# Late stores, longer rings and streamed filler operands in a four-layer training step

## The chip, the cores and the metric

The kernel runs on one core of a Trainium2 chip. The metric is the device time of one launch in microseconds (us). All executions used here are of the fast state; the program uses one core. Times are medians of the executions.

Engine names: PE is TensorE (matmul), PEld its weight loads, DVE is VectorE, ACT is ScalarE, POOL is GpSimd, SP is SyncE, which issues the loads. A `q` behind a name (SPq) is that engine's sequencer.

## The reference, cut to what matters

One forward and one backward pass over four residual layers: linear attention, gated GLU, linear attention, gated GLU. Sequence 2048, width 512, GLU width 1376, bf16. Both attention layers share weights, and both GLU layers do.

```python
x = x + A(layernorm(x), wqkv, wo)             # layer 0
x = x + B(layernorm(x), w_gate, w_up, w_down) # layer 1
x = x + A(layernorm(x), wqkv, wo)             # layer 2
x = x + B(layernorm(x), w_gate, w_up, w_down) # layer 3
# A: phi(t) = where(t > 0, t + 1, exp(t)) + 1e-6, 32 heads of 16
#    kv = phi(k)^T v;  z = sum phi(k);  o = phi(q) kv / (phi(q) z + 1e-6);  y = o @ wo
# B: h = sigmoid(x @ w_gate) * (x @ w_up);  y = h @ w_down
out, vjp = jax.vjp(f, x, wqkv, wo, w_gate, w_up, w_down);  grads = vjp(grad_out)
```

## The kernel before

The kernel works in blocks of four 128-row tiles (512 rows), four blocks in all. Its stages, in order: first attention forward (a key loop, then a query phase), first GLU forward, second attention forward, a fused forward and backward of the last GLU, backward attention 2, backward of the first GLU, backward attention 0, and the final weight gradients. In the backward stages, weight gradients of layers already finished serve as *filler*: their matmuls have low priority and go where TensorE would wait.

Three parts matter. First, the key loop. A pair tile `pkst` (ring of 2) feeds a transposing transfer into `pkT`, of which there is only one; the store of `pkT` is issued by GpSimd in program order:

```python
k.work, k.p_pq, k.p_st, k.p_M = pool("work", 2), pool("pq", 2), pool("stage", 2), pool("M", 1)
...
    if st % 2 == 0:
        k.pkst = k.p_st.tile([P, 2, D], BF16, name="pkst")
    ...
    if j == 0:
        k.pkT = k.p_st.tile([P, NB, NDC, P], BF16, name="pkT", bufs=1)
    if st % 2:
        nc.sync.dma_start_transpose(out=k.pkT[:, j - 1:j + 1]..., in_=flat(k.pkst))
    if j == NB - 1:
        k.st.dma_start(out=sv["pkT"][b], in_=flat(k.pkT))       # k.st is GpSimd
```

Second, the query phase. It divides by the denominator as exp(-ln d). VectorE makes `qp`, GpSimd makes `rp`, and GpSimd issues the stores of `qp`, `rp` and of the transposed `qn`:

```python
nc.scalar.activation(ld[:], d_ps[:], ACT.Ln, bias=k.eps[:])
nc.scalar.activation(rd[:], ld[:], ACT.Exp, scale=-1.0)
nc.vector.tensor_tensor(qp[:, dc, :], pq[:, dc, :], rd[:], ALU.mult)
nc.gpsimd.tensor_tensor(rp[:, dc, :], eq[:, dc, :], rd[:], ALU.mult)
```

Third, the filler weight gradients. Each sum over 16 row tiles needs a natural operand (`g_all` or `h_all`, kept whole in memory, 2 MB) and a transposed one (`set_t`, loaded block by block through a transposing transfer):

```python
def mid2():
    k.g3 = load_all(k, sv[3]["g"], "g_all"); wd3(SETS[0:1])
def mid0():
    dw_cols(k, "wqkv", D, (0, D), [(k.h2, sv[2]["dkT"])], "first")
    k.h3 = load_all(k, sv[3]["h"], "h_all")
a_bwd(k, 2, False, hi, mid2)
wd3(SETS[1:])
k.h2 = load_all(k, sv[2]["h"], "h_all")
with hi():
    b_bwd(k, 1)
dw_cols(k, "wqkv", 0, (0, D), [(k.h2, sv[2]["dqT"])], "first")
a_bwd(k, 0, True, hi, mid0)
...
for st, t in pieces(k, src, c0, w):            # t: a set_t tile's rows
    for ic in range(NDC):
        matmul(ps[ic], lhsT=h[:, st, ic * P:(ic + 1) * P], rhs=t, ...)
```

Of the kernel before, what the change touches and what calls it, by code (L numbers as in the profile page):

```python
# [16 lines left out]
D = 512  # L17
# [38 lines left out]
def kernel(  # L56
# [60 lines left out]
    k.A = {l: {} for l in (0, 2)}  # L117

# [55 lines left out]




class LN:
# [11 lines left out]
    def one(self, st):  # L190
# [12 lines left out]
        nc.gpsimd.tensor_tensor(rstd, rstd, k.neghalf[:], ALU.pow)  # L203
# [8 lines left out]
        if j == NB - 1:  # L212
            k.st.dma_start(out=by_tile(k.sv[l]["h"], b * NB, NB), in_=self.h[b][:])
            if l % 2 == 0:
                k.st.dma_start(out=k.sv[l]["hT"][b], in_=flat(self.hT[b]))
# [11 lines left out]
def forward(k):  # L227
    nc, tc = k.nc, k.tc
    with ExitStack() as ctx:
# [19 lines left out]
        b_both(k, 3, lns[3])  # L249

# [42 lines left out]
def a_fwd(k, l, ln, nxt):  # L293
    with ExitStack() as ctx:
        pool = lambda name, bufs, **kw: ctx.enter_context(k.tc.tile_pool(name=f"{name}{l}", bufs=bufs, **kw))
        k.work, k.p_pq, k.p_st, k.p_M = pool("work", 2), pool("pq", 2), pool("stage", 2), pool("M", 1)
# [14 lines left out]
def a_fwd_body(k, l, ln, nxt):  # L311
# [10 lines left out]
    def keys(st):  # L322
        b, j = divmod(st, NB)
        hT = ln.hT[b][:, j]
        if st % 2 == 0:
            k.pkst = k.p_st.tile([P, 2, D], BF16, name="pkst")
# [8 lines left out]
        pk = k.pkst[:, st % 2, :]  # L335
        pks.append((pk, nc.vector.scalar_tensor_tensor(pk, k_ps[:], 1.0 + EPS, a_t[:], ALU.add, ALU.max)))  # L336
        if j == 0:
            k.pkT = k.p_st.tile([P, NB, NDC, P], BF16, name="pkT", bufs=1)
        if st % 2:
            nc.sync.dma_start_transpose(out=k.pkT[:, j - 1:j + 1].rearrange("p a c q -> p (a c) q"), in_=flat(k.pkst))  # L340
        if j == NB - 1:
            k.st.dma_start(out=sv["pkT"][b], in_=flat(k.pkT))
# [58 lines left out]
    for b in range(NBLK):  # L401
        pq, eq = qb[b]
        qp = qps[b] = k.p_st.tile([P, NDC, SB], BF16, name="qp_t")
        rp = k.p_st.tile([P, NDC, SB], BF16, name="rp_t", bufs=1)
        for dc in range(NDC):
# [7 lines left out]
            nc.gpsimd.tensor_tensor(rp[:, dc, :], eq[:, dc, :], rd[:], ALU.mult)  # L413
        k.st.dma_start(out=sv["qp"][b], in_=flat(qp))
        k.st.dma_start(out=sv["rp"][b], in_=flat(rp))
        qn = k.p_st.tile([P, NDC, NB, P], BF16, name="qn_t", bufs=1)
        nc.sync.dma_start_transpose(out=qn[:].rearrange("p c a q -> p (c a) q"), in_=flat(qp))
        k.st.dma_start(out=sv["qn"][b], in_=flat(qn))
        if b + 2 < NBLK:
            qb.append(q_block(k, ln.hT[b + 2]))  # L420
        if b:
            out(b - 1)
    out(NBLK - 1)

    k2_ps = k.ps.tile([P, NDC, P], F32, name="kv_ps", tag="bank")
    for c in range(NDC):
        mm4(k, k2_ps[:, c, :], lambda ic: Eb(ic, c), lambda ic: wv(ic, c))
    nc.vector.tensor_tensor(kv[:], k2_ps[:], mask4, ALU.mult)
    MT = k.keep.tile([P, NDC, D], BF16, name=f"MT{l}")
    for jc in range(NDC):  # L430
        m_ps = k.ps.tile([P, D], F32, name="MT_ps", tag="bank")
        for c in range(NDC):
            nc.tensor.matmul(m_ps[:, c * P:(c + 1) * P], lhsT=k.wo[:, c, jc * P:(jc + 1) * P], rhs=kvT[:, c, :],
                             start=True, stop=True)
        (nc.vector.tensor_copy if jc % 2 else nc.scalar.copy)(MT[:, jc, :], m_ps[:])
    A.update(nz=nz, kv=kv, MT=MT)


def b_fwd(k, l, ln, nxt):
    nc, sv = k.nc, k.sv[l]  # L440
    with ExitStack() as ctx:
# [12 lines left out]
        for b in range(NBLK):  # L454
            ln.need(b * NB + NB - 1)
            hT = ln.hT[b]
            hhT = hhs[b] = p_hh.tile([P, NFC, SB], BF16, name="hhT_t")
            for f0, nf in FGRP:
                s4 = p_s.tile([P, 4, SB], BF16, name="s_t")
                for fc in range(f0, f0 + nf):  # L460
# [8 lines left out]
                    if fc == 3:  # L469
                        ln.need((b + 2) * NB - 1)  # L470
# [5 lines left out]
        down(NBLK - 1)  # L476


def b_both(k, l, ln):

    nc, sv = k.nc, k.sv[l]
    with ExitStack() as ctx:
# [3 lines left out]
        hhs, dds, gns, gTs = {}, {}, {}, {}  # L486

        def grads(b):
            gns[b] = k.p_h.tile([P, NB, D], BF16, name="gn_t", tag="h_t")
            nc.sync.dma_start(out=gns[b][:], in_=by_tile(k.g_in, b * NB, NB))  # L490
            gTs[b] = k.p_hT.tile([P, NDC, SB], BF16, name="gT3_t", tag="hT_t")
            nc.sync.dma_start_transpose(out=gTs[b][:], in_=k.g_in[rows(b * NB, NB), :])
# [12 lines left out]
        grads(0)  # L505
        for b in range(NBLK):
# [3 lines left out]
            for fc in range(NFC):  # L510
# [28 lines left out]
                if fc == 3 and b + 1 < NBLK:  # L539
                    grads(b + 1)  # L540
                    ln.need((b + 2) * NB - 1)
# [24 lines left out]
def backward(k):  # L566
    nc, tc = k.nc, k.tc
    with ExitStack() as ctx:
# [3 lines left out]
        k.small = pool("bsmall", 6, side="right")  # L572
        k.p_all = pool("dw_all", 2, side="right")
# [394 lines left out]
```

## Time and profile before

The kernel before takes 1333.15 us (three runs, 1331.93 to 1333.93).

| what | value | view |
|---|---|---|
| span of the profiled run | 1334.9 us | page |
| TensorE busy | 1128.9 us | page, busy list |
| all matmuls at the warm pace | about 1038 us | worked out, see below |
| mean granted clock | 0.932 | cores |
| DMA traffic | 236.25 MB, mean 177 GB/s | page |

The page's busy list, and its slices. Each slice is 1/40 of the span, each digit a busy share in tenths; PEclk is the clock granted to TensorE in tenths, DMA the mean share of the 16 transfer engines.

```profile
PE 1128.9 (85%) x5254; PEld 514.1 (39%) x5344; DVE 606.8 (45%) x1103; ACT 390.6 (29%) x769; POOL 388.9 (29%) x548
PE   3675789988579999998789769888978978899997
PEclk9888799998789999999889799988989989999999
DMA  9846554464778334146964898454575568976994
```

TensorE is busy 85% of the span, with low digits in the first five slices and again in slices 11 and 12: these are the two attention forwards. The next lines are two of GpSimd's waits from 16 to 137 us (who waited for whom, us in total, times, longest).

```profile
POOL sv_pkT_109 L342 <- DMA pkT<-pkst: 19.3, 2, 11.3
POOL sv_qn_112 L418 <- DMA qn_t<-qp_t: 16.6, 3, 11.4
```

GpSimd stands 19.3 us in front of stores whose source, a transposed tile, has not landed, and 16.6 us in front of stores of `qn`. VectorE waits too, for the transfer that still reads `pkst` (VectorE's waits, 16 to 75 us):

```profile
DVE pkst L336 <- DMA pkT<-pkst: 12.6, 3, 5.0
```

In the query phases the table of windows gives busy time by engine: us of the window, then busy us and instruction counts of PE, PEld, DVE, ACT and POOL, the granted clock, the DMA share and GB/s.

```profile
74.00:137.00 63.00, 39.91 (x194) 17.54 (x196) 45.15 (x87) 30.65 (x51) 27.64 (x34) 0.84 0.53 142
316.00:372.00 56.00, 40.02 (x200) 17.88 (x202) 44.85 (x86) 30.38 (x51) 25.21 (x31) 0.85 0.69 188
```

Last, a piece of the chain of waits in the GLU backward (start, us, what). "Issue" is time in which the profile shows nothing being waited for; VectorE's next step, at 819.02 us, stands behind it.

```profile
792.15 26.88 issue
```

### The profile page before, as it was taken

What the parts mean: (1) busy time and instruction counts of PE and PEld (TensorE: products, weight loads), DVE (VectorE), ACT (ScalarE), POOL (GpSimd) and SP (SyncE); (2) the same over time, 40 slices, a digit from 0 to 9 for tenths busy, and PEclk for the clock granted to TensorE, in tenths of its full rate; (3) what the DMA queues carried; (4) which work ended last, traced back from release to release, by engine and by line L of the source; (5) the groups of instructions that cost most, each with busy time, mean ns of one, the idle gap of its engine ahead of it and who ended that gap; (6) DMA issues with size and microseconds to landing.
All of it is one profiled execution on the core that took longest, in us unless ns stands there. A gap on an engine that the chain in (4) does not pass through costs nothing. (4 is left out here: it accounts for less than half of the span.)

```text
span 1334.9 us, 14969 instructions
## 1 busy us (share of the span) xinstructions
PE 1128.9 (85%) x5254; PEld 514.1 (39%) x5344; DVE 606.8 (45%) x1103; ACT 390.6 (29%) x769; POOL 388.9 (29%) x548
## 2 busy tenths in 40 slices
PE   3675789988579999998789769888978978899997
PEld 1232333433234444443344324333434433345543
DVE  6277465446774545445547411555634851000011
ACT  1153321214535335243212532545221340000000
POOL 7134343211565344241320142334132111000111
PEclk9888799998789999999889799988989989999999
DMA  9846554464778334146964898454575568976994
GB/s 267 239 142 142 142 164 139 160 177 110 220 183 245 95 124 131 61 144 155 279 209 156 217 237 256 154 179 133 151 212 198 195 155 176 232 168 135 235 252 114
DMA packets 377420, 236.25 MB, mean 177 GB/s; under 512 B 290945, under 2 KB 352193, under 8 KB 377345
## 3 DMA queue, kind: packets, MB, share of 16 engines
q1 hardware_dynamic: 355968, 163.32, 49.5%
q0 software_dynamic: 21376, 71.97, 14.9%
q8 instruction: 42, 0.69, 0.2%
q14 instruction: 34, 0.27, 0.1%
HBM read 69.60 MB, written 94.50 MB: 123 GB/s over the span
## 5 line engine op out<-in xcount | busy, mean ns | idle before, releaser
L920 PE MATMUL dw_ps<-set_t,h_all 128*128 128x512 bf16 (+1 forms) x1006 | 210.0, 366 | 10.1 <-DMA set_t<-sv_ddT_130 4.4
L920 PEld LDWEIGHTS <-h_all 128*128 128x128 bf16 x1024 | 100.6, 99 | 115.4 <-issue 16.4
L891 DVE TENSOR_TENSOR dw_new<-dw_ps,dw_old 128x512 bf16<-128x512 f32 (+1 forms) x27 | 17.4, 686 | 221.4 <-PE dw_ps L920 151.5
L159 PE MATMUL g_ps<-hT_t,wg 128*128 128x512 bf16 x352 | 96.8, 399 | 13.1 <-DMA hT_t<-h_t 8.3
L159 PE MATMUL dhh_ps<-gT_t,wdT 128*128 128x512 bf16 x339 | 93.0, 394 | 14.0 <-ACT dhh_t L681 5.6
L159 PE MATMUL u_ps<-hT_t,wu 128*128 128x512 bf16 x352 | 94.8, 392 | 0.0
L893 ACT CAST dw_new<-dw_ps 128x512 bf16<-128x512 f32 (+2 forms) x51 | 26.5, 573 | 222.3 <-PE dw_ps L920 107.1
L683 DVE TENSOR_TENSOR dd_t<-dhh_t,sh_t 128x1024 bf16<-128x1024 bf16 x44 | 40.7, 938 | 110.4 <-ACT dhh_t L681 39.9
L894 POOL DMA_DIRECT2D out_dram<-dw_new x51 | 27.5, 542 | 213.9 <-ACT dw_new L893 122.0
L654 PE MATMUL dh_ps<-wuT,dd_t 128*128 128x512 bf16 x169 | 65.9, 391 | 20.1 <-ACT t_sb L622 16.0
L934 PE MATMUL dw_ps<-g_all,set_t 128*128 128x512 bf16 (+1 forms) x342 | 79.3, 383 | 4.2 <-ACT dw_new L893 2.0
L521 POOL TENSOR_TENSOR sd_t<-hh_t,oms 128x512 bf16<-128x512 bf16 x44 | 51.8, 1178 | 92.1 <-DVE hh_t L520 74.6
L724 POOL TENSOR_TENSOR dqT_t<-w_t,rp_l 128x512 bf16<-128x512 bf16 x32 | 37.5, 1188 | 128.1 <-DVE w_t L723 51.3
L654 PE MATMUL dh_ps<-wgT,dd_t 128*128 128x512 bf16 x173 | 67.2, 389 | 0.4
L353 PE MATMUL E_ps<-pkst,h_t 128*128 128x512 bf16 x125 | 40.4, 455 | 27.2 <-DVE pkst L336 27.2
L654 PEld LDWEIGHTS <-dd_t 128*128 128x128 bf16 x352 | 35.0, 100 | 65.5 <-issue 24.4
L527 DVE TENSOR_TENSOR dd_t<-dhh_t,sd_t 128x1024 bf16<-128x1024 bf16 x44 | 34.9, 798 | 53.1 <-POOL sd_t L521 53.1
L159 PEld LDWEIGHTS <-wdT 128*128 128x128 bf16 x352 | 35.4, 101 | 59.0 <-issue 20.6
L159 PEld LDWEIGHTS <-wg 128*128 128x128 bf16 x352 | 35.7, 102 | 58.3 <-issue 20.7
L159 PEld LDWEIGHTS <-wu 128*128 128x128 bf16 x352 | 35.7, 101 | 45.5 <-issue 7.0
L934 PEld LDWEIGHTS <-set_t 128*128 128x128 bf16 (+1 forms) x352 | 35.3, 101 | 46.3 <-issue 7.6
L465 ACT ACTIVATE s_t<-g_ps 128x512 bf16<-128x512 f32 x44 | 25.7, 598 | 87.9 <-PE g_ps L159 74.9
(608 smaller groups left out, 1974.8 us busy)
## 6 DMA issues: line engine op xcount, KB each, us to landing
sv_ddT_130<-dd_t SPq DMA_DIRECT2D x40, 256.0 KB, 2.2
sv_ddT_116<-dd_t SPq DMA_DIRECT2D x40, 256.0 KB, 2.5
out_dram<-dw_new POOLq DMA_DIRECT2D x42, 128.0 KB, 3.8
sv_hhT_115<-hhT_t POOLq DMA_DIRECT2D x4, 1280.0 KB, 6.1
sv_hhT_129<-hh_t POOLq DMA_DIRECT2D x40, 128.0 KB, 2.2
sv_s_118<-s_t POOLq DMA_DIRECT2D x8, 512.0 KB, 4.7
out_dram<-o_t POOLq DMA_DIRECT2D x16, 256.0 KB, 2.5
sh_t<-sv_s_118 SPq DMA_DIRECT2D x8, 512.0 KB, 5.1
```

Source lines behind the costliest of these rows:

```text
L159: i = k.nc.tensor.matmul(out, lhsT=lhs(c), rhs=rhs(c), start=(c == 0), stop=(c == n - 1))
L353: nc.tensor.matmul(E_ps[ic][:], lhsT=h[:, ic * P:(ic + 1) * P], rhs=pk, start=(st == 0), stop=(st == NST - 1))
L465: k.last_sigmoid = nc.scalar.activation(s4[:, fc - f0, :], g_ps[:], ACT.Sigmoid)
L521: nc.gpsimd.tensor_tensor(sd[:, 1, :], hh[:], oms[:], ALU.mult)
L527: mul = nc.vector.tensor_tensor(dd[:], dhh[:].unsqueeze(1).to_broadcast([P, 2, SB]), sd[:], ALU.mult)
L654: nc.tensor.matmul(acc[b][j][:], lhsT=dd[:, a, rows(j)], rhs=(k.wuT, k.wgT)[a][:, fc, :], start=(fc == 0 and a == 0), stop=(fc == NFC - 1 ...
L683: nc.vector.tensor_tensor(dd[:], dhh[:].unsqueeze(1).to_broadcast([P, 2, SB]), sh[:, :, i, :], ALU.mult)
L724: nc.gpsimd.tensor_tensor(dqT[:, dc, :], w_t[:], rp[:, dc, :], ALU.mult)
L893: nc.scalar.copy(new[0:r, 0:w], ps)
L894: k.st.dma_start(out=dst, in_=new[0:r, 0:w])
L920: k.nc.tensor.matmul(ps[ic][:, 0:w], lhsT=h[:, st, ic * P:(ic + 1) * P], rhs=t, start=(i == 0 and st == 0), stop=(i == len(srcs) - 1 and s ...
L934: k.nc.tensor.matmul(p[0:r, :], lhsT=t[:, f:f + r], rhs=g[:, st, :], start=(i == 0 and st == 0), stop=(i == len(srcs) - 1 and st == NST - 1))
```

## The change

Its intent, in four parts:

1. Key tiles, transposed keys, `qp`, `rp` and `qn` come from one ring of 7 tiles of 4 KB per partition, not from rings of 2 and 1.
2. A store of a transposed tile (`pkT`, `hT`, `qn`) is put later in GpSimd's program order, behind four more of its reciprocal products or layer-norm steps, so GpSimd does useful work while the transpose lands. The small products of the attention (`kv`, `MT`) move into the query loop, and layer norms and output gradients are asked for earlier.
3. In the backward stages `qp`, `rp` and the GLU's `s`/`hhT` loads share one ring `sh` that lives through all stages; `dqT` has two tiles in place of one.
4. The filler gradients no longer keep a whole natural operand: both operands are streamed block by block through a ring of 6 set tiles. Filler is cut into smaller pieces and none is left inside the GLU backward. The staging ring grows from 2 to 3. For the final gradients the ring of set tiles stays at 6, where before it had 8 there.

```diff
+def pooled(k, ins):
+    k.n_pool += 1
+    while k.waiting and k.waiting[0][0] <= k.n_pool:
+        after(k, k.st.dma_start(**k.waiting.pop(0)[1]), ins)
+def store_later(k, lag=4, **kw):
+    k.waiting.append((k.n_pool + lag, kw))
 ...
-    k.work, k.p_pq, k.p_st, k.p_M = pool("work", 2), pool("pq", 2), pool("stage", 2), pool("M", 1)
+    k.work, k.p_pq, k.p_st, k.p_M = pool("work", 2), pool("pq", 2), pool("stage", 7), pool("M", 1)
 ...
-            k.st.dma_start(out=sv["pkT"][b], in_=flat(k.pkT))
+            store_later(k, out=sv["pkT"][b], in_=flat(k.pkT))
 ...
-        rp = k.p_st.tile([P, NDC, SB], BF16, name="rp_t", bufs=1)
+        rp = k.p_st.tile([P, NDC, SB], BF16, name="rp_t", tag="st")
 ...
-            nc.gpsimd.tensor_tensor(rp[:, dc, :], eq[:, dc, :], rd[:], ALU.mult)
+            pooled(k, nc.gpsimd.tensor_tensor(rp[:, dc, :], eq[:, dc, :], rd[:], ALU.mult))
 ...
-        k.p_all = pool("dw_all", 2, side="right")
-        k.p_set, k.p_dst, k.p_ln = mpool("dw_set", 4), mpool("dw_stage", 2), mpool("lnb", 2)
+        k.p_set, k.p_dst = pool("dw_set", 6), pool("dw_stage", 3)
+        k.p_sh, k.p_ln = mpool("sh", 2), mpool("lnb", 2)
 ...
+        wd3 = lambda i: dw_rows(k, "wd", SETS[i], [(sv[3]["g"], sv[3]["hhT"])], "first")
+        dqk2 = lambda i: dw_cols(k, "wqkv", i * D, (0, D), [(sv[2]["h"], sv[2][("dqT", "dkT")[i]])], "first")
+        a_bwd(k, 2, False, hi, lambda: wd3(0))
         with hi():
             b_bwd(k, 1)
+        wd3(1)
+        a_bwd(k, 0, True, hi, lambda: dqk2(0))
+        dqk2(1)
+        wd3(2)
+        mctx.close()
+        k.p_all, k.p_dst = pool("dw_all", 2), pool("dw_stage_end", 6)
+        h3, h1 = load_all(k, sv[3]["h"], "h_all"), load_all(k, sv[1]["h"], "h_all")
 ...
-            qp = ph1.tile([P, NDC, SB], BF16, name="qp_l")
-            rp = ph1.tile([P, NDC, SB], BF16, name="rp_l", bufs=1)
+            qr = k.p_sh.tile([P, 2, NDC, SB], BF16, name="qr_l", tag="sh")
 ...
     for b in range(NBLK):
+        if len(nat.shape) == 2:
+            n = k.p_set.tile([P, NB, D], BF16, name="nat_t", tag="set_t")
+            k.nc.sync.dma_start(out=n[:], in_=by_tile(nat, b * NB, NB))
         t = k.p_set.tile([P, NB, w], BF16, name="set_t", tag="set_t")
         k.nc.sync.dma_start_transpose(out=t[:], in_=src[c0:c0 + w, b * SB:(b + 1) * SB])
```

## The prediction

> **What bounds it now.** TensorE, through waits. The page's busy list gives PE 1128.9 us of 1334.9. Back-to-back 128x512 matmuls start 0.216 us apart in the timeline of the fused GLU stage (400 to 617 us); all 5344 matmuls at that pace would take about 1040 us (my estimate). So about 290 us are lost: 206 idle, the rest matmuls at the low clock after a gap (634 ns instead of 379). That agrees with the Trainium skill, "TensorE: Matmul & The Clock Gate", Part 1: an idle window of about 3.4 us halves the clock. A removed gap pays more than its length.
>
> Weight-load starts in the timeline against that pace give the loss by stage: first attention forward, to 155 us: 85; first GLU forward, to 270: 15; second attention forward and hand-over, to 402: 51; fused GLU, to 617: 3; backward attention 2: 18 + 9; hand-over to the GLU backward (742 to 822): 31; rest of it, to 938: 25; backward attention 0: 24; final weight gradients with their hand-over: 26.
>
> **What the change does on the critical path.**
> 1. Key features: two pair tiles and one transposed tile become a ring of 7. Waits before: VectorE 18.5 us for transposes still reading the tile, PE 27.2 us for VectorE, GpSimd 19.3+17.0 us holding a store of transposed keys. The first key loop took from 26 to 74 us for 25 us of matmul. Its last input transposes land only at 45, so it can end near 53: 20 to 25 us, and 6 to 8 the second time.
> 2. Late stores: the store of transposed queries held GpSimd 17.7+14.0 us; behind it stood the reciprocal products, ScalarE (13.1 us) and the layer norm. With the MT products inside the loop (8.2 us wait for ScalarE at 128 to 137), earlier layer norms and gradient loads: 12 to 15 us first, 15 to 20 second, 5 in the GLU forward. DMA limits this: its share is 0.85 from 16 to 75 us.
> 3. Backward rings: dqT and rp were single; GpSimd waited 13.0+13.5 us for rp loads and 21 for dqT stores, then VectorE, then PE. About 6 + 8. Against it: the order puts the first load of block 0 behind six loads and the 8.2 us transpose of wqkv, so attention 2 may begin 5 us late.
> 4. Hand-over to the GLU backward: ScalarE stood 27 us (792 to 819) in a copy of a weight gradient whose matmuls were filler, while the stage's own copies waited. The order has no filler inside this stage now, and its first loads stand ahead of the attention part. About 20.
> 5. GLU backward block ends (three stalls of 5 to 6 us plus slow clock): order unchanged, no gain.
> 6. End: deeper staging, filler moved: about 8. Streaming both operands adds about 6 MB of loads, off the path.
>
> Sum about 110 us; I take off 15 for contention and for waits that appear behind those removed: 1240 us, 8 in 10 between 1203 and 1282. Chances: faster 0.94, same 0.05, slower 0.01.
>
> **What would show it.** First key loop ends before 58 us with no VectorE wait for key transposes; GpSimd's waits on key and query stores vanish; no ScalarE stand over 10 us at the start of the GLU backward; its three block-end stalls remain; PE busy falls towards 1090.
>
> **What would make it wrong.** DMA saturation in the first 110 us, so that removed waits return as slow landings; late first loads in backward attention 2; a stall when the final operands are loaded into just-freed memory.

## The result, and the profile after

After: 1308.41 us (four runs, 1307.86 to 1309.67), beside 1332.54 us before (1331.29 to 1333.93). The ratio is 0.982, 95% interval 0.9803 to 0.9837. A ratio here is the mean time of one kernel's fast runs over that of the other's fast runs of the same rounds, so it is not quite the ratio of the medians. Predicted were 1240 us with a range of 1203 to 1282 and faster by over 2%: both are wrong.

The same lines of the page after. Busy TensorE time fell to 1116.9 us, not towards 1090. Slices 2 and 5 (counting from 1) are fuller; slices 32 and 33 (7 and 5, before 9 and 7) are emptier, and the DMA share there is now 9.

```profile
PE 1116.9 (86%) x5256; PEld 509.9 (39%) x5344; DVE 619.5 (47%) x1103; ACT 391.1 (30%) x769; POOL 390.5 (30%) x548
PE   2975999886599999988897778796889759999987
PEclk8988999997799999999998888998989889999999
DMA  9959455648892532376948945447863999776994
```

To see where time went, I cut both traces at the same matmuls and compare, for each stage, the time between those weight loads with the time that the matmuls between them need at full pace (columns divided by 2.4 per ns: 512 columns in 0.213 us). The Trainium skill, "TensorE: Matmul & The Clock Gate", Part 1, gives this pace plus about 2.5 ns per matmul, 215.7 ns for 512 columns; the trace's starts are 0.216 us apart, so it agrees. What a stage took beyond that I call its loss.

| stage | before: took / loss | after: took / loss | loss saved |
|---|---|---|---|
| attention 0, keys | 57.9 / 31.4 | 39.2 / 12.7 | 18.7 |
| attention 0, queries | 63.5 / 30.2 | 54.6 / 21.3 | 8.9 |
| first GLU forward | 137.3 / 23.0 | 130.3 / 15.9 | 7.1 |
| attention 2, keys | 41.4 / 14.9 | 33.9 / 7.5 | 7.4 |
| attention 2, queries | 55.5 / 22.2 | 61.4 / 28.1 | -5.9 |
| fused last GLU | 243.4 / 16.4 | 240.8 / 13.8 | 2.6 |
| backward attention 2, first part | 72.0 / 23.3 | 60.6 / 20.1 | 3.2 |
| backward attention 2, second part | 60.3 / 4.0 | 61.5 / 4.7 | -0.7 |
| its end and GLU backward | 189.7 / 56.1 | 166.0 / 48.7 | 7.4 |
| backward attention 0, first part | 88.6 / 20.5 | 84.8 / 24.8 | -4.3 |
| backward attention 0, second part | 59.7 / 3.4 | 60.7 / 4.0 | -0.6 |
| its end and final weight gradients | 240.1 / 25.9 | 286.1 / 40.4 | -14.5 |

The stages took other times partly because filler moved between them; only the losses compare. The forward half saved 38.8 us. The backward half lost 9.5 us, although points 3, 4 and 6 of the prediction were to save 42 (37 with the 5 us that point 3 takes off).

In the first attention the waits that were to vanish did. What is left of them from 16 to 137 us after:

```profile
POOL sv_qn_112 L181 <- DMA qn_t<-qp_t: 3.4, 1, 3.4
```

The waits for a landing transpose went from 19.3 + 16.6 us to 3.4 us, and VectorE has no wait for a key tile left. In the second query phase they did not vanish: one store of `qn` still holds GpSimd for 8.7 us, where two had held it for 5.9 us. And the query phases, and the end of the backward pass, look like this in the windows:

```profile
55.00:110.00 55.00, 41.77 (x200) 17.94 (x201) 48.05 (x85) 32.99 (x55) 30.12 (x37) 0.88 0.72 194
274.00:336.00 62.00, 40.83 (x200) 17.85 (x201) 50.78 (x92) 32.77 (x54) 31.59 (x39) 0.85 0.74 196
1010.00:1030.00 20.00, 14.24 (x85) 6.79 (x85) 5.21 (x9) 6.22 (x13) 4.20 (x8) 1.00 0.92 213
1030.00:1050.00 20.00, 16.64 (x66) 7.06 (x67) 2.76 (x4) 2.15 (x4) 4.07 (x8) 0.83 1.01 259
1050.00:1075.00 25.00, 11.65 (x42) 4.76 (x41) 0.69 (x1) 2.14 (x4) 2.91 (x6) 0.79 1.12 320
```

Two things are to be seen. In the query phases VectorE's busy time *rose*, from 45.15 to 48.05 us (85 instructions against 87) and from 44.85 to 50.78 us (92 against 86). The mean of one `qp` product rose from 644 to 888 ns in the first and from 558 to 721 ns in the second. And from 1010 to 1075 us the transfers take 0.92 to 1.12 of what the 16 engines have, at 213 to 320 GB/s, while TensorE runs filler with gaps, from 1030 us on at a lower clock. (A packet's whole time is put in the window in which it starts, so a share can pass 1.) (The Trainium skill, "DMA: Bandwidth & Descriptors", Latency and other measured facts, gives 261 GB/s as the effective rate of a transposing transfer with a non-contiguous middle dimension; the mix of plain and transposing loads here spans that figure.) TensorE's timeline there, with the idle time before each group and what ended it:

```profile
1032.11 4.68 PE L927 MATMUL dw_ps<-set_t,nat_t 128*128 128x512 bf16 x10 [4.67 <-ACT dw_new L896]
1073.57 8.78 PE L927 MATMUL dw_ps<-set_t,h_all 128*128 128x512 bf16 x28 [9.82 <-DMA set_t<-sv_ddT_130]
```

The last one, 9.82 us, waits for the first transposed tile of the final gradients. The queue that issues the loads (SyncE's sequencer) shows why it is late: seven loads of whole operands stand ahead of it.

```profile
1057.02 2.05 SPq L903 DMA_DIRECT2D h_all<-sv_h_128  x3
1059.11 4.32 SPq L903 DMA_DIRECT2D h_all<-sv_h_114  x4
1063.53 7.73 SPq L914 DMA_TRANSPOSE set_t<-sv_ddT_130  x1
```

### The profile page after: what moved, and what is told of

The parts are those of the page before. It is cut to its first block, busy times and chain, and to the rows that moved or that the text cites. A ratio compares the mean times of both kernels' runs of the same rounds, so it can differ in the third digit from the quotient of the medians.

```text
span 1306.1 us, 14957 instructions
## 1 busy us (share of the span) xinstructions
PE 1116.9 (86%) x5256; PEld 509.9 (39%) x5344; DVE 619.5 (47%) x1103; ACT 391.1 (30%) x769; POOL 390.5 (30%) x548
## 2 busy tenths in 40 slices
DMA packets 383756, 242.54 MB, mean 186 GB/s; under 512 B 291137, under 2 KB 358529, under 8 KB 383681
## 4 chain that ended last, share of the span: by engine, by line
PE 41%; issue 24%; DVE 8%; DMA 8%; POOL 5%; ACT 2%; SPq 2%; POOLq 0%; DVEq 0%; ACTq 0%
PE dh_ps L573 6%; PE g_ps L161 6%; PE u_ps L161 6%; PE y_ps L161 5%; PE dhh_ps L161 5%; PE dh_ps L843 3%; PE dh_ps L657 3%; POOL out_dram L897 2%; PE dpk_ps L161 2%; DMA sh_t<-sv_hhT_115 2%; POOL sh_t L682 1%; DVE u_t L759 1%; SPq L914 1%; PE E_ps L367 1%; DVE u_t L728 1%
## 5 line engine op out<-in xcount | busy, mean ns | idle before, releaser
L927 PE MATMUL dw_ps<-set_t,h_all 128*128 128x512 bf16 (+1 forms) x883 | 179.5, 363 | 14.6 <-DMA set_t<-sv_ddT_130 9.8
L894 DVE TENSOR_TENSOR dw_new<-dw_ps,dw_old 128x512 bf16<-128x512 f32 (+1 forms) x27 | 17.4, 686 | 267.3 <-PE dw_ps L927 186.7
L927 PEld LDWEIGHTS <-h_all 128*128 128x128 bf16 x896 | 88.1, 98 | 106.0 <-DMA set_t<-sv_ddT_130 10.3
L686 DVE TENSOR_TENSOR dd_t<-dhh_t,sh_t 128x1024 bf16<-128x1024 bf16 x44 | 39.2, 899 | 86.7 <-ACT dhh_t L684 52.0
L727 POOL TENSOR_TENSOR dqT_t<-w_t,qr_l 128x512 bf16<-128x512 bf16 x32 | 38.3, 1207 | 88.5 <-DVE w_t L726 88.2
L657 PEld LDWEIGHTS <-dd_t 128*128 128x128 bf16 x352 | 35.1, 101 | 67.4 <-issue 23.3
L941 PEld LDWEIGHTS <-set_t 128*128 128x128 bf16 (+1 forms) x352 | 36.7, 106 | 60.6 <-issue 16.6
L941 PE MATMUL dw_ps<-nat_t,set_t 128*128 128x512 bf16 (+1 forms) x171 | 49.4, 434 | 11.5 <-DMA set_t<-sv_hhT_129 8.6
L161 PEld LDWEIGHTS <-wu 128*128 128x128 bf16 x352 | 35.1, 100 | 43.7 <-issue 3.9
L573 PEld LDWEIGHTS <-dd_t 128*128 128x128 bf16 x352 | 34.4, 98 | 41.5
L161 PE MATMUL k_ps<-wqkv,hT_t 128*128 128x512 bf16 x124 | 35.0, 409 | 16.4 <-DMA hT_t<-h_t 16.2
```

The lines of the kernel that those rows point to most:

```text
L161: i = k.nc.tensor.matmul(out, lhsT=lhs(c), rhs=rhs(c), start=(c == 0), stop=(c == n - 1))
L573: k.nc.tensor.matmul(dh_ps[:], lhsT=dds[fc][:, a, rows(j)], rhs=(k.wuT, k.wgT)[a][:, fc, :], start=(i == 0), stop=(i == 2 * NFC - 1))
L657: nc.tensor.matmul(acc[b][j][:], lhsT=dd[:, a, rows(j)], rhs=(k.wuT, k.wgT)[a][:, fc, :], start=(fc == 0 and a == 0), stop=(fc == NFC - 1 ...
L686: nc.vector.tensor_tensor(dd[:], dhh[:].unsqueeze(1).to_broadcast([P, 2, SB]), sh[:, :, i, :], ALU.mult)
L727: nc.gpsimd.tensor_tensor(dqT[:, dc, :], w_t[:], rp[:, dc, :], ALU.mult)
L927: k.nc.tensor.matmul(ps[ic][:, 0:w], lhsT=h_t[:, ic * P:(ic + 1) * P], rhs=t, start=(i == 0 and st == 0), stop=(i == len(srcs) - 1 and st ...
```

## The experiments

Seventeen kernels ran. The kernel after was timed only beside its own runs of before; so kernels are compared through their ratio to before, where after stands at 0.982. One per cent is about 13 us.

| kernel | median us (runs' range) | ratio to before, 95% |
|---|---|---|
| fwd_only | 1298.17 (1294.59 to 1305.12) | 0.9757 (0.9715 to 0.9798) |
| bwd_only | 1342.26 (1339.83 to 1347.13) | 1.0086 (1.0049 to 1.0123) |
| lazy_h | 1297.38 (1295.43 to 1300.57) | 0.9739 (0.9703 to 0.9776) |
| stage4 | 1306.99 (1301.82 to 1315.85) | 0.9823 (0.9772 to 0.9875) |
| nat_once (wrong result) | 1290.05 (1284.67 to 1294.40) | 0.9660 (0.9627 to 0.9693) |
| no_later | 1319.73 (1318.42 to 1320.71) | 0.9883 (0.9864 to 0.9903) |
| rp_dve | 1296.35 (1289.39 to 1301.15) | 0.9721 (0.9688 to 0.9754) |
| rings | 1308.25 (1305.86 to 1314.82) | 0.9806 (0.9774 to 0.9838) |
| res1 | 1289.92 (1281.76 to 1296.49) | 0.9653 (0.9596 to 0.9710) |
| fwd_rp | 1281.97 (1280.11 to 1283.55) | 0.9596 (0.9558 to 0.9634) |
| before_rp | 1327.51 (1326.00 to 1328.93) | 0.9937 (0.9904 to 0.9969) |
| best_all | 1267.03 (1262.70 to 1272.01) | 0.9486 (0.9439 to 0.9532) |
| gt_ring | 1306.69 (1301.00 to 1309.70) | 0.9799 (0.9770 to 0.9828) |
| wq_order | 1304.74 (1299.21 to 1307.11) | 0.9786 (0.9756 to 0.9816) |
| grads_late | 1308.18 (1300.27 to 1311.96) | 0.9807 (0.9773 to 0.9840) |
| hand2 | 1299.31 (1292.87 to 1305.46) | 0.9748 (0.9712 to 0.9785) |
| best_wqs | 1261.23 (1258.78 to 1264.68) | 0.9463 (0.9434 to 0.9492) |

### Which half gains: fwd_only and bwd_only

Edit: only the hunks of the diff that lie in the forward pass, or only those in the backward pass.

> The kernel before with the forward part of the change alone (ring of 7, late stores, MT inside the loop, early layer norms and gradient loads); the backward is the old one. By the two traces the changed kernel ends its forward 38.7 us earlier than before and takes 10 us longer over the backward. Theory A (the stages add up, the backward part of the change is itself the loss): about 1294 us, faster than the whole change. Rival B (the forward gain is borrowed: stores put off there come back as slower loads later, whatever the backward looks like): about 1305 to 1310 us.

> The old forward with the backward part of the change alone. Theory A: 1340 to 1345 us, slower than before by about 10. Rival B: the backward part pays as I predicted (about 50 us) when the forward does not disturb it: about 1285 us; or it is at least faster than 1330.

The forward half alone reaches 0.9757, faster than the whole change; the backward half alone is a loss, 1.0086. In fwd_only the end of the forward pass comes at the time it has in after, and the end and final gradients lose 23.4 us (after: 40.4; before: 25.9). The backward half moved time from stage to stage and then paid for it at the end.

### Loads at first use: lazy_h

The edit, abridged; a further line asks for a block of the natural operand just ahead of the transposed tile that it goes with.

```diff
-def load_all(k, src, name):        # four block loads at once
-    t = k.p_all.tile([P, NST, D], BF16, name=name, tag="all")
-    for b in range(NBLK): k.nc.sync.dma_start(out=t[:, b * NB:(b + 1) * NB, :], ...)
+class load_all:                    # a block is loaded when it is first used
+    def __getitem__(self, at):
+        b = at[1] // NB
+        if b not in self.done: self.done.add(b); self.k.nc.sync.dma_start(...)
+        return self.t[at]
```

> The changed kernel, but the natural operands of the last weight gradients are loaded block by block, each just ahead of the transposed piece that it goes with, in place of eight loads in front of the first piece. Theory (the 9.8 us wait of PE at 1064 to 1074 us is the first transposed piece standing behind seven 512 KB loads in the one queue): that wait falls under 3 us and the kernel gains 8 to 11 us, about 1298 us. Rival (the loads are bound by bandwidth: the memory only came free at 1057 us and the same bytes must arrive): the wait moves to later pieces and the gain is under 4 us.

It runs at 0.9739, about 11 us under after. The one wait of 9.8 us became five of 5.1 us together (TensorE's waits from 1010 us to the end):

```profile
PE dw_ps L936 <- DMA set_t<-sv_ddT: 5.1, 5, 2.6
```

The rival was right in part: TensorE's waits for the filler's `hhT` tiles in the same stretch rose from 3.6 to 8.4 us. The loss of the end and the final gradients fell from 40.4 to 35.1 us, and did not reach before's 25.9: the order of loads is one part of the cost at the end, not all. The 5.3 us saved there are also only half of the 11 us, whose interval is about 5 us to each side. From 1060 to 1090 us TensorE was busy 24.86 of 30 us at full clock with a DMA share of 1.08, so a full DMA share alone doesn't stop TensorE.

### Deeper staging: stage4

```diff
-    new = pool.tile([P, D], BF16, name="dw_new")
+    new = pool.tile([P, D], BF16, name="dw_new", **({} if pool is k.p_dst else dict(bufs=4)))
-        old = pool.tile(..., **({} if pool is k.p_dst else dict(bufs=1)))
+        old = pool.tile(..., **({} if pool is k.p_dst else dict(bufs=4)))
```

> The changed kernel with four staging tiles in place of two (new) and one (old) for the weight gradients that the attention stages write themselves. Theory (in-order queues: a load of the old gradient waits for the one tile, and the filler's operands stand behind it in the queue at 1015 to 1050 us; ScalarE's copies wait for the two staging tiles' stores at 719 to 725 us, and the first matmuls of the GLU backward behind them): waits for set tiles in 1010 to 1060 us and the 1.3+2.1+3.3 us at 719 to 725 us vanish, 10 to 14 us gained, about 1296 us. Rival (the filler streams both operands and is bound by DMA in these 50 us): gain under 4 us, the waits for set tiles stay.

My theory fell here. The end of backward attention 2 took 19.7 us in place of 23.5, but the whole kernel stayed at 0.9823; the old partial gradients were now loaded early and the same stretch of filler waited for its set tiles instead. Here a wait removed inside a congested stretch returned as another.

### The streamed operand: nat_once and res1

nat_once loads the natural operand of each filler for block 0 only and reuses the tile. The matmuls stay; the gradients are wrong.

```diff
-        if len(nat.shape) == 2:
+        if len(nat.shape) == 2 and b == 0:
```

> The kernel after, but the filler gradients (three sets of wd of layer 3, dq and dk parts of wqkv of layer 2) load the natural operand for the first block only and reuse that tile for all four; their results are wrong on purpose, 7.5 MB less are loaded, every matmul stays. Theory A (streaming both operands makes the unhidden filler at the end of backward attention 0 bound by the DMA: 63.5 us for 34.3 us of matmul there, DMA share 0.9 to 1.1): that stretch falls to 42 to 50 us, the stretch of backward attention 0 before it by 2 to 5 us, and the whole kernel by 12 to 20 us to about 1290. Rival B (the loss there comes from the order of loads in one issuing queue and from the old partial gradients, not from bytes): under 5 us, 1304 to 1308.

It took 1290.05 us, ratio 0.9660: about 21 us less than after. But not where I had said. The end stretch went from 63.5 to 55.1 us, less than expected; the first part of backward attention 0 went from 84.8 to 72.7 us, much more. The two windows of that part, after and then nat_once:

```profile
864.00:949.00 85.00, 67.45 (x340) 30.76 (x344) 46.47 (x92) 21.14 (x43) 24.47 (x24) 0.94 0.69 204
862.00:935.00 73.00, 63.08 (x335) 29.57 (x341) 44.96 (x91) 20.80 (x43) 24.73 (x24) 1.00 0.70 206
```

The DMA share is 0.69 and 0.70. So in this stage the transfers were not saturated, and "bound by bytes" is not what the lines say. A filler that streams two operands also fills the ring of 6 with three blocks' pairs and puts twice as many loads into the one queue, ahead of the stage's own. Which of these weighed most there is not separated. In before the same part lost 20.5 us with the natural operand whole in memory.

res1 is a version with right results: the natural operand is whole in memory again, but one at a time, in one buffer. All three filler sets of `wd` come first, then the two parts of layer 2's `wqkv`, so the order of the filler and the rings of set tiles (4, and 5 at the end) change too.

```diff
+        k.p_all = pool("dw_all", 1)
-        k.p_set, k.p_dst = pool("dw_set", 6), pool("dw_stage", 3)
+        k.p_set, k.p_dst = pool("dw_set", 4), pool("dw_stage", 3)
+        g3 = lambda: ops.get("g3") or ops.setdefault("g3", load_all(k, sv[3]["g"], "g_all"))
+        h2 = lambda: ops.get("h2") or ops.setdefault("h2", load_all(k, sv[2]["h"], "h_all"))
-        a_bwd(k, 0, True, hi, lambda: dqk2(0))
-        dqk2(1)
-        wd3(2)
+        a_bwd(k, 0, True, hi, lambda: wd3(2))
+        dqk2(0)
+        dqk2(1)
```

> The kernel after, with the filler gradients' natural operand kept whole in memory again, but in one buffer instead of two: the layer 3 gradient is loaded once for all three wd sets, which now all come before the dq and dk parts, and then layer 2's h once for both of those; the ring of set tiles goes back from 6 to 4 and every result is right. It loads 7.5 MB less minus 0 extra, like the run with the reused tile. Theory A (bytes): 1288 to 1298, most of what the reused tile gained (its 1290). Rival B (the reused tile gained from its shorter queue of loads and freer ring, and a correct version cannot): 1303 to 1310.

It took 1289.92 us, ratio 0.9653, the time that the theory said; that bytes are the cause does not follow, since order and rings changed with them. (The expectation's "7.5 MB less" is wrong: the pages show 242.54 MB after and 236.25 MB in before and in res1, so 6.3 MB.) The loss of backward attention 2's two parts fell from 24.8 to 18.0 us and that of backward attention 0's first part from 24.8 to 17.0; the end's loss stayed, at 39.9, because its bulk loads still came in a lump.

### Late stores alone: no_later

```diff
 def store_later(k, lag=4, **kw):
-    k.waiting.append((k.n_pool + lag, kw))
+    k.st.dma_start(**kw)
```

> The kernel after, with every late store issued at once where before issued it; the ring of 7 staging tiles stays. Theory A (the ring, not the lateness, ended the key waits; but GpSimd stands behind each store of a transpose not yet landed, as it did before, and the layer norms and reciprocal products with it): the key loops lose 3 to 8 us each and the query phases 3 to 6 us together, the kernel 8 to 20 us slower than after, 1316 to 1328. Rival B (with a ring, a store that waits costs nothing that matters because the next work has slack): within 4 us of after.

It took 1319.73 us, ratio 0.9883, about 8 to 11 us slower than after. The key loops were the same as in after (39.7 and 33.7 us against 39.2 and 33.9), which the expectation missed: the key waits end without the lateness, so it is the ring that ended them. The lateness pays in the first query phase (59.2 us in place of 54.6), the first GLU forward (135.5 in place of 130.3) and the fused stage (243.4 in place of 240.8). In the second query phase it pays nothing in sum (61.7 in place of 61.4): GpSimd stood 21.0 us before stores of `qn` there, but the wait for the late transposed layer norm (see grads_late) is absent.

### VectorE and GpSimd: rp_dve, fwd_rp and before_rp

In the query phase of after, GpSimd's product `rp` and VectorE's work overlap like this (timeline, other engines left out; start, us, engine, line, operation, count, idle before):

```profile
67.62 0.43 DVE L426 TENSOR_TENSOR qp_t<-pq_t,rd_t 128x512 bf16<-128x512 bf16 x1
67.67 1.39 POOL L427 TENSOR_TENSOR rp_t<-eq_t,rd_t 128x512 bf16<-128x512 bf16 x1 [7.96 <-ACT rd_t L425]
67.96 1.38 DVE L301 TENSOR_SCALAR a_t<-eq_t 128x1024 bf16<-128x1024 bf16 x1
...
69.63 2.27 POOL L427 TENSOR_TENSOR rp_t<-eq_t,rd_t 128x512 bf16<-128x512 bf16 x2
70.58 1.61 DVE L426 TENSOR_TENSOR qp_t<-pq_t,rd_t 128x512 bf16<-128x512 bf16 x1
```

One `qp` product, begun just before GpSimd's, takes 0.43 us; the next, begun while GpSimd works, takes 1.61 us; `a_t`, 0.43 us at other times, takes 1.38 us and ends just after the GpSimd product does. The Trainium skill, "SBUF — State Buffer", SBUF: two separate sides, says that VectorE and GpSimd share one pair of ports, which a GpSimd instruction, or a VectorE instruction in a two-port mode or with two SBUF inputs, locks for its whole length. The edit takes the product off GpSimd:

```diff
-            pooled(k, nc.gpsimd.tensor_tensor(rp[:, dc, :], eq[:, dc, :], rd[:], ALU.mult))
+            pooled(k, nc.vector.tensor_tensor(rp[:, dc, :], eq[:, dc, :], rd[:], ALU.mult))
```

> The kernel after, with the reciprocal product rp moved from GpSimd to VectorE in both attention forwards (32 products of 1.2 us leave GpSimd, 32 of about 0.4 us alone are added to VectorE). Theory A (the query phases are bound by VectorE, and part of its busy time is waiting for GpSimd's products to release the SBUF port, as the Trainium skill, SBUF - State Buffer, states and as a 128x1024 tensor_scalar of 0.43 us that took 1.38 us beside a product at 68 us suggests): VectorE's qp products fall from a mean of 0.72 and 0.89 us to 0.4 to 0.5, its busy time in each query phase falls or stays, and each phase becomes 2 to 6 us shorter; the kernel 4 to 12 us faster. Rival B (no shared port; the mean of those products is a modelled end): VectorE's busy time rises by 6 us in each query phase, each phase is 2 to 6 us longer, the kernel 4 to 12 us slower.

It took 1296.35 us, ratio 0.9721: about 13 us less than after, although VectorE was given 32 more products. The groups of VectorE (line, shapes, count, busy us, mean ns), after first:

```profile
L426 DVE TENSOR_TENSOR qp_t<-pq_t,rd_t 128x512 bf16<-128x512 bf16 x32 | 25.4, 806 | 1.8 <-ACT rd_t L425 1.1 <-issue 0.7
L301 DVE TENSOR_SCALAR a_t<-eq_t 128x1024 bf16<-128x1024 bf16 x16 | 8.8, 549 | 0.3
```

and in rp_dve:

```profile
L427 DVE TENSOR_TENSOR rp_t<-eq_t,rd_t 128x512 bf16<-128x512 bf16 x32 | 13.3, 418 | 0.0
L426 DVE TENSOR_TENSOR qp_t<-pq_t,rd_t 128x512 bf16<-128x512 bf16 x32 | 13.2, 416 | 1.6 <-ACT rd_t L425 1.6
L301 DVE TENSOR_SCALAR a_t<-eq_t 128x1024 bf16<-128x1024 bf16 x16 | 6.9, 432 | 0.3
```

The mean of `qp` fell from 806 to 416 ns. VectorE does `qp` and `rp` in 26.5 us, where `qp` alone had taken 25.4 us beside GpSimd. The products cost GpSimd 1.2 us each. Its windows in the two query phases:

```profile
56.00:109.00 53.00, 41.15 (x208) 18.63 (x210) 46.67 (x105) 33.03 (x55) 11.48 (x22) 0.90 0.77 202
266.00:320.00 54.00, 42.07 (x205) 18.71 (x207) 45.53 (x104) 32.55 (x54) 12.05 (x23) 0.87 0.79 212
```

VectorE's busy time is lower than in after, with more instructions in it. The losses went from 21.3 to 17.4 us (first query phase), from 28.1 to 19.1 us (second) and from 15.9 to 10.8 us (first GLU forward). TensorE's wait of 7.5 us for the last transposed layer norm at the end of the second query phase is gone in this run. That wait is most of the 9.0 us saved there, and its cause is another (see grads_late). What the 13 us owe to VectorE's shorter products, and what to a GpSimd that is free sooner for stores and layer norms, the run does not separate.

fwd_rp puts the same edit on fwd_only, before_rp on before.

> The forward half of the change alone (backward as before) plus the reciprocal product on VectorE. If the two gains add (forward half 34 us below before, the product 12 us below after): 1282 to 1290. If the gain of the product overlaps with that of the forward half (waits that only move): 1294 to 1300.

> The kernel before with the one edit of the reciprocal product on VectorE. Theory A (in before GpSimd stands in stores and VectorE has slack in the query phases; with the product off GpSimd the chain from GpSimd's stand to the reciprocal ring is shorter, but the stores still hold the layer norms): 3 to 10 us faster, less than the 12 us it gave on after. Rival B (the port alone matters, whatever the stores do): 11 to 16 us faster. Rival C (only worth something once the stores are gone): within 3 us.

fwd_rp took 1281.97 us, ratio 0.9596: the gains add. before_rp took 1327.51 us, ratio 0.9937 or about 8 us, against 13 us on after. The intervals of these two gains overlap, so that the product's cost was partly hidden behind GpSimd's stands in before, as Theory A has it, is not shown. In before_rp the first query phase took 58.7 us in place of 63.5, but the second 60.0 in place of 55.5.

### Gradient loads and the second query phase: grads_late

The edit, with comments added:

```diff
-        if b == 2 and l == 2:
-            last_grads(k, 0)          # in the query loop
+        last_grads(k, 0)              # at the start of the fused stage, as in before
```

> The kernel after, with the loads of block 0 of the output gradient back at the start of the fused GLU stage, as in before. Theory A (the early gradient loads stand ahead of the last transposed layer norm in the queue and cost the second query phase its stall of 7.5 us): that phase takes 54 to 57 us where it took 61.4, the fused stage no longer, the kernel 3 to 7 us faster. Rival B (the phase is bound by VectorE and its products' waits for GpSimd, as the run with the product on VectorE says; the load stall only stands in front): 59 to 63 us, within 2 us.

The kernel stayed where it was (ratio 0.9807), the phase took 65.2 us, and the stall was there and longer, 10.2 us (TensorE's waits, 270 to 345 us):

```profile
PE g_ps L161 <- DMA hT_t<-h_t: 10.2, 1, 10.2
```

But Theory A was not tested. The issuing queue of after, then of grads_late, shows the transposed loads of the gradients (`gT_t`; the second of two is shown) still ahead of the last transposed layer norm (`hT_t`): the scheduler put the loads back where they were.

```profile
322.14 7.47 SPq L498 DMA_TRANSPOSE gT_t<-in_grad_out_dram  x1
329.67 3.77 SPq L223 DMA_TRANSPOSE hT_t<-h_t  x1
```

```profile
320.58 6.46 SPq L496 DMA_TRANSPOSE gT_t<-in_grad_out_dram  x1
327.08 6.24 SPq L223 DMA_TRANSPOSE hT_t<-h_t  x1
```

In rp_dve, where the wait is gone, the layer norm goes ahead of the second gradient load:

```profile
309.80 1.52 SPq L223 DMA_TRANSPOSE hT_t<-h_t  x1
311.42 6.65 SPq L498 DMA_TRANSPOSE gT_t<-in_grad_out_dram  x1
```

In after the layer norm's last row tile is written at 319.8 us, but its transfer is issued only at 329.7 and lands at 335.6 us. In the eleven kernels that have after's forward pass, grads_late among them, the phase took 58.4 to 66.2 us and TensorE's wait for this transfer 4.5 to 11.9 us; the phase less the wait is 53.9 to 55.0 us in all of them. In before it took 55.5 us without such a wait. So what this phase lost against before is this one wait. With the product on VectorE and the rest of after's forward pass the phase took 52.1 to 54.1 us in four kernels, without the wait. The order alone is not the whole cause: in before, too, both gradient loads stood ahead of this transfer, but they held the queue for 5.3 us together, where in after they held it for 15.6 us. Why they took longer in after no run shows.

### Backward attention 2's first loads: rings and wq_order

rings meant two things: the transposed load of `wqkv` one block later, and `dqT` in a ring of its own, so that no later tile lies over it. The edit, without the line that makes this ring:

```diff
-            if b == 0 and l == 2:
+            if b == 1 and l == 2:
                 nc.sync.dma_start_transpose(out=k.wqkvT[:], in_=k.w_in["wqkv"])
-            dqT = ph1.tile([P, NDC, SB], BF16, name="dqT_t")
+            dqT = k.p_dq.tile([P, NDC, SB], BF16, name="dqT_t")
```

> The kernel after, with the transposed load of wqkv issued one block later in backward attention 2 and with the two dqT tiles of each backward attention in a ring of their own that the later dkvT tile does not overlay. Theory A (the 5.4 us wait of TensorE at 589 us is the first qp and rp load standing behind that transpose, and the waits of 4.7 and 3.9 us of the Wp matmuls are dkvT waiting for the last store of dqT): all three waits vanish, attention 2 backward loses 8 to 10 us and attention 0 backward 3 to 4 us of their time, the kernel 8 to 13 us faster. Rival B (these waits only stand in front of others, filler takes the place): the waits move and the kernel changes by less than 4 us.

It gained nothing (0.9806). Its queue shows that the first half was not tested: the transposed load still stands ahead of the first `qr_l` load, as in after, because the scheduler placed it there. The second half was tested: the 4.7 and 3.9 us waits of the `Wp` matmuls went, and waits of 2.9 us for the copies before them, twice, came in their place. wq_order forces the order with an edge:

```diff
+            rp_ld = nc.sync.dma_start(out=rp..., in_=sv["rp"][b])
-                nc.sync.dma_start_transpose(out=k.wqkvT[:], in_=k.w_in["wqkv"])
+                after(k, nc.sync.dma_start_transpose(out=k.wqkvT[:], in_=k.w_in["wqkv"]), rp_ld)
```

> The kernel after, with an ordering edge that puts the transposed load of wqkv behind the first qp and rp loads of backward attention 2 in the issuing queue (the run called rings meant to do this and left the order as it was). Theory A (predicted: that transpose holds the first loads and costs about 5 us): TensorE's wait of 5.4 us at 589 us vanishes and the kernel is 3 to 7 us faster. Rival B (the loads wait for memory or for the bandwidth of the forward's last loads, so they land as late): within 2 us.

The issuing queue in after, then in wq_order:

```profile
576.84 6.99 SPq L751 DMA_TRANSPOSE wqkvT<-in_A_wqkv_dram  x1
584.18 0.35 SPq L746 DMA_DIRECT2D qr_l<-sv_qp_124  x1
```

```profile
578.45 0.35 SPq L746 DMA_DIRECT2D qr_l<-sv_qp  x1
579.38 8.30 SPq L751 DMA_TRANSPOSE wqkvT<-in_A_wqkv_dram  x1
```

TensorE's wait there fell from 5.4 to 1.9 us, the stage's loss from 20.1 to 18.4 us. The kernel is at 0.9786, whose interval (0.9756 to 0.9816) just reaches into that of after. So the transposed load did delay the first loads; that the whole kernel gains from the new order is not shown.

### The hand-over to the GLU backward: gt_ring and hand2

```diff
-        k.p_sh, k.p_ln = mpool("sh", 2), mpool("lnb", 2)
+        k.p_sh, k.p_ln, k.p_gt = mpool("sh", 2), mpool("lnb", 2), mpool("gt", 2)
-            g_t = k.p_h.tile([P, NB, D], BF16, name="g_t", tag="h_t")
+            g_t = k.p_gt.tile([P, NB, D], BF16, name="g_t")
```

> The kernel after, with the gradient tiles that enter the GLU backward in a ring of two of their own, where they shared a ring of four with the loads of the attention backward. Theory A (the hand-over kept about 6 us because ScalarE stands in such a copy for a transpose that frees a shared tile, and TensorE's first C matmul behind it): the wait of 6.0 us of the C matmuls for ScalarE vanishes, the stretch from the first C matmul to the end of the GLU backward takes 160 us or less where it took 166, and the kernel is 4 to 8 us faster. Rival B (behind it stand the two staging tiles of the weight gradients and the first loads): the wait moves, less than 3 us.

hand2 is gt_ring with four staging tiles where backward attention 2 stores its weight gradients.

> The kernel after, with the own ring for the gradient tiles and with four staging tiles in place of two for the weight gradients that close backward attention 2. Theory A (two waits stand one behind the other: copies of the gradient, then staging tiles whose stores have not landed): the stretch from the first C matmul to the end of the GLU backward falls from 166 us (165.5 with the ring alone) to 154 to 159, and the kernel is 5 to 11 us faster than after. Rival B (a third wait follows, the first loads of the GLU backward or the clock): that stretch stays over 162 us, the kernel within 4 us.

Three of TensorE's waits from the first C matmul to the end of the GLU backward, in after:

```profile
PE C_ps L859 <- ACT t_sb L625: 6.0, 1, 6.0
PE dh_ps L657 <- DVE dd_t L686: 3.8, 4, 1.8
PE dhh_ps L161 <- ACT dw_new L896: 3.3, 1, 3.3
```

With gt_ring the first line is gone and the last one reads:

```profile
PE dhh_ps L161 <- ACT dw_new L896: 8.4, 1, 8.4
```

The wait moved, and the stretch took 165.5 us against 166.0. With hand2 both are gone or small:

```profile
PE dh_ps L657 <- DVE dd_t L686: 8.2, 4, 4.5
PE dhh_ps L161 <- ACT dw_new L896: 2.2, 1, 2.2
```

The stretch took 160.1 us, and the kernel runs at 0.9748, about 10 us under after. The kernel's gain is the one that Theory A gave; the stretch lies between the two theories: two waits stood one behind the other, and part of a third (8.2 us where it was 3.8) came up behind them. Neither edit alone gained: gt_ring is at 0.9799, and stage4, which has four staging tiles there too but not the ring, at 0.9823.

### A version that beats both: best_all and best_wqs

best_all is the kernel after with res1's resident operands, rp_dve's product and lazy_h's loads. best_wqs adds wq_order's edge and the four staging tiles.

> The three remedies together on the kernel after: natural operands of the fillers resident in one buffer, the reciprocal product on VectorE, and whole-operand loads issued block by block at first use. If they add: 12 (product) + 12 to 18 (resident) + 5 to 10 (loads), 1268 to 1282. If the last two act on the same congested stretch and overlap: 1278 to 1290.

> The best version so far (resident operands, product on VectorE, loads block by block; 1267 us) with the ordering edge for the first loads of backward attention 2 and the four staging tiles. If these add: 1257 to 1263. If they only move waits: 1264 to 1270.

best_all took 1267.03 us (0.9486), best_wqs 1261.23 us (0.9463); both give right results. The last two edits together are worth about 3 us by the ratios, within the intervals. The page of best_wqs shows a busy TensorE of 1108.7 us in a span of 1259.5 us:

```profile
PE 1108.7 (88%) x5344; PEld 507.8 (40%) x5344; DVE 606.3 (48%) x1135; ACT 389.5 (31%) x769; POOL 351.9 (28%) x516
```

What remains is the start (a wait of 16.0 us for the first transposed tile), the three block-end stalls of the GLU backward (17.1 us in three), and the first block of the fused stage (11.9 us).

## Why the prediction was wrong, point by point

| point of the prediction | predicted saving | measured |
|---|---|---|
| 1. keys | 20 to 25, and 6 to 8 | 18.7, and 7.4 |
| 2. first query phase | 12 to 15 | 8.9 |
| 2. second query phase | 15 to 20 | -5.9 |
| 2. GLU forward | 5 | 7.1 (and 2.6 in the fused stage) |
| 3. backward attention 2, first part | 6, less 5 | 3.2 |
| 3. backward attention 0, first part | 8 | -4.3 |
| 4. hand-over to the GLU backward | 20 | 7.4 |
| 5. block ends | 0 | 0: three stalls of 5 to 6 us remain |
| 6. end | 8, and loads "off the path" | -14.5 |

**Keys: right.** The loop ends at 55.4 us (predicted near 53, and before 58), with no wait of VectorE for a key tile. no_later keeps the ring, issues the stores at once, and its key loops are as short: the ring did this and not the lateness of the stores.

**First query phase: the mechanism was right, its size was not.** GpSimd's stands shrank to 3.4 us, and no_later shows what lateness is worth: 8 to 11 us in the whole kernel, 4.6 us in this phase. The step that failed is "the store ... held GpSimd; behind it stood the reciprocal products", taken as if those waits could be subtracted. VectorE was the busiest engine there before the change, at 45 us, and GpSimd's freed products then met VectorE's more often: one `qp` product took 888 ns in place of 644. rp_dve shows what this costs: with the product off GpSimd the phase loses 3.9 us less, and the first GLU forward 2 to 5 us less (10.8 us, where the kernels with after's forward pass lost 13.0 to 16.2; the fused stage lost 2 us more). The busy line that would have said so was in the table of windows.

**Second query phase: the steps that failed are that the late stores would pay here as well, and "earlier ... gradient loads" as part of the saving.** The lateness paid nothing in sum (no_later, 61.7 against 61.4 us): by the traces, what it saved on GpSimd's stands went into the wait for a late transfer. The last transposed layer norm was issued behind two transposed gradient loads that held the queue for 15.6 us, and TensorE waited 7.5 us for it, more than the 5.9 us that the phase lost. Here the order is read from the queues of all the kernels; no run changed it by itself.

**The late first load of backward attention 2: right.** It cost 5.4 us of TensorE's wait, 1.9 us once the order was forced (wq_order).

**Hand-over: the step that failed is "About 20", read from ScalarE's 27 us.** It named a stand from 792 to 819 us; the trace shows one VectorE product waiting 27.0 us behind weight-gradient copies, while ScalarE itself worked at intervals. The window of before over just this stretch gives TensorE busy 21.89 of 27 us, at full clock:

```profile
792.00:819.00 27.00, 21.89 (x96) 9.64 (x97) 0.15 (x1) 7.63 (x13) 10.46 (x13) 1.00 0.88 220
```

It was mostly doing filler (64 of the 96 matmuls in that window). Only about 5 us were TensorE's, and a wait of another engine is worth only the idle time of the bottleneck in it. So most of the 31 us that the prediction had counted as lost from 742 to 822 us lay before that stand, from 742 to 792. Two waits from there were left after the change, 6.0 and 3.3 us (4.2 and 3.2 before); gt_ring and hand2 show them one behind the other.

**End: the failed step is "Streaming both operands adds about 6 MB of loads, off the path".** The 6 MB are right (242.54 against 236.25 MB). They were not off the path: without the repeated loads (nat_once) the kernel is about 21 us faster, with a resident operand (res1) about 22 us. A part of the loss I had not looked for lies earlier, in backward attention 0's first part, where the ring's predicted 8 us came out as -4.3; without the repeated loads the loss there falls from 24.8 to 13.2 us, below before's 20.5 by 7.3 us, about the 8 that was predicted. The loads of the final operands, in a lump ahead of the first tile that was needed, cost another 5.3 us at the end (lazy_h; 11 us in the whole kernel, give or take 5). Of the 14.5 us lost at the end, nat_once gives back about 8 and lazy_h 5; whether the shorter ring of set tiles there (6 in place of 8) has a part in it no run tested. The prediction had listed "a stall when the final operands are loaded into just-freed memory" as a risk; it gave it no number.

**Allowance.** I took 15 us off for contention and waits behind waits. These took about 23 us in the query phases with the GLU forward, 13 us at the hand-over, 12 us in backward attention 0 and 22 us at the end (predicted less measured, with the middle of each range), of the sum of about 110.

**What stays open.** Which of bytes, ring slots and queue order made streaming dear in backward attention 0, where the DMA share was 0.69. And why the two transposed gradient loads held the queue for 15.6 us in the second query phase, where they had held it for 5.3 us before.

## What to carry to other kernels

Before subtracting a wait, read the bottleneck engine's busy time in that window and the busiest engine's: a 27 us stand in which TensorE was busy 22 us is worth 5, and a phase in which VectorE is busy 45 us cannot shrink below that unless this busy time itself falls. After an edit that is meant to move a load, look at the issuing queue: in rings and in grads_late the scheduler had left it where it was. Here filler was free only while its operands arrived: keeping a 2 MB operand whole for several sums that share it was worth about 22 us (give or take 8), and letting each block be loaded where it is first used about 11 (give or take 5). Where VectorE is the busiest engine, a two-input product given to GpSimd "to help" can cost VectorE as much time as doing the product itself.

## What the Trainium skill lacked or had wrong

- "SBUF — State Buffer", SBUF: two separate sides: the exclusive lock is stated and these runs agree, but it gives no time for a mix of bf16 products of this size. Here 32 GpSimd products of 1.2 us raised VectorE's 128x512 bf16 product from a mean of 416 to 806 ns and a 128x1024 tensor_scalar from 432 to 549 ns, while the operation that reads PSUM and SBUF (`pq_t`) stayed at 684 against 683 ns.
- "GPSIMD Engine Reference", 4.1 Engine selection: it gives about 2 times slower for two-input elementwise work. For 128x512 bf16 these runs show 1216 ns on GpSimd (after) against 418 ns on VectorE (rp_dve), 2.9 times (the page's own measurement is of fp32 operands; the GpSimd figure is taken beside a working VectorE, its shortest is 1140 ns); and VectorE needed 26.5 us for `qp` and `rp` together where `qp` alone had taken 25.4 us beside GpSimd.
- No page that I read puts a number on a store issued from GpSimd whose source has not landed, with GpSimd's own compute behind it: 19.3 us for two stores of keys and 16.6 us for three of `qn` in before.
- "DMA: Bandwidth & Descriptors", Latency and other measured facts: it has a rate for transposing transfers but none for a mix with plain transfers, for which these runs show 213 to 320 GB/s at a DMA share of 0.92 to 1.12, nor how long a transposing load takes to land in such a mix: two of 512 KB took 6.2 us (median) in before and 12.7 us in after, both at a DMA share of 1.0 or more.
